# Two value visits of the last head group joined into one burst, with gate loads and softmax sums set behind it

## The chip, the cores and the metric

The kernel runs on one core of one Trainium2 chip. The metric is the device time of one execution in microseconds (us). In the profile's rows PE is TensorE, PEld its weight loads, DVE VectorE, ACT ScalarE, POOL GpSimd and SP the queue that issues nearly all transfers.

## What is computed

One input x of 2048 tokens by 512 goes through two blocks, which a gate per token mixes. Block a is attention with 32 heads of 16 in a causal window of 256 tokens; block b is a gated linear unit with inner size 1376.

```python
def _A_ref(x, wqkv, wo):
    ...
    scores = jnp.einsum("bhqd,bhkd->bhqk", q, k) * (Dh ** -0.5)
    mask = (idx[:, None] - idx[None, :] >= 0) & (idx[:, None] - idx[None, :] < W)
    scores = jnp.where(mask[None, None], scores, -1e9)
    p = _softmax(scores, axis=-1)
    o = jnp.einsum("bhqk,bhkd->bhqd", p, v)
    return (lambda x, *d: x.transpose(*d))(o, 0, 2, 1, 3).reshape(B, S, D) @ wo

def _B_ref(x, w_gate, w_up, w_down):
    ...
    h = _sigmoid(g) * u
    return jnp.einsum("bsf,fd->bsd", h, w_down)

g = _sigmoid((x * gate_w).sum(-1, keepdims=True))
return g * a + (1 - g) * b
```

## The kernel before

Every fp32 product is made of fp32r products of a high and a low part: high by high, high by low, low by high.

**Steps.** The 32 heads are 8 groups of 4, the tokens 16 blocks of 128. One long loop runs over `u` from 0 to 137, a step for each block of each group (group 7 has u 112 to 127) and a few to drain. The order on every engine but POOL is the order in which this code is written. In a step, for each head `hh` of the four: `s_part` (L370) makes a score product of block u with up to two blocks before it, and VectorE takes its row maxima (L376, an instruction and a read-out); nine steps later (`LAG`) `st_part` (L425) makes the transposed scores, with the maxima folded in as extra rows, and ScalarE takes their exponentials (L430) into a buffer, where POOL clears the masked corners (L436, L442). The score products of two heads run side by side in the two halves of TensorE's rows. They end with u 127, the transposed ones with u 136.

**Maxima.** Each four steps the maxima of a chunk of 512 tokens are turned by `max_split` on VectorE (L386, L387, L391), stored, and loaded back by `max_load` into rows of the `ring`, from which the transposed products read them.

**Fillers.** Between the score products stand halves of other products, in pairs side by side as well: projections of the next groups, then the gate and up products (`gu`, L282), and from about u 121 the tail products (`tp`, L612), the last columns of the gate and up matrices and the mixing gate. How many pairs follow each head's scores is read from `GAPS2` (the groups with long bursts) and `GAPS`. ScalarE copies a gate product out; of a tail group VectorE takes a transpose and a copy (L618, L619).

**Value visits.** At step u, `pv_part` (L460) multiplies the exponentials of one chunk with the values, in four column tiles of 32 for the four heads; its 17th row per head is the softmax sum. `visits[u]` is 2 for a long burst of two chunks (chunks of seven head groups, at u 17, 25, to 121) and 1 for single visits (u 125, 129, 133, 137, the last group). A single visit's result is copied out by ScalarE in `o_take` (L471). In a long burst `o_copy` (L478) copies the first half from the bank "pv" and the second from a bank of the tag "st", of which there are two and which the transposed products use in turn; then `o_store` puts the stores in `later`, a list that the next step hands to the SP queue.

**Homes of the exponentials.** `p_home` says where a block's exponentials lie: groups with long bursts use `pbuf` and `pwide`, the last group `pbuf` alone. `pwide` shares its memory with `hv`, the buffer of the gate and up products that come back from DRAM (`h_load`, L757) for the last stage.

**Guests.** `behind` and `acts` hold small work for VectorE and ScalarE that is put in at chosen heads: splits of the down matrix (L136 on ScalarE, L137, the low part, on VectorE) and of wo, and the reciprocals of the softmax sums. `SUMS` says after which step the sums of a chunk are read back (L821), `H_LOAD` when the first gate chunks are.

**The last stage** takes h = sigmoid(g)·u from those chunks (L811, L812), multiplies by the down matrix and by wo, mixes and stores. Its TensorE work is dense and starts behind the tail products.

Of the kernel before, what the change touches and what calls it, by code (L numbers as in the profile page):

```python
# [24 lines left out]
NB = T // P  # L25
# [14 lines left out]
LAG = 9  # L40
PVLAG = LAG + 4
WIDE = 2 * 4
NWIDE = NG - 1
# [3 lines left out]
GAPS = [3] * 12 + [2] * 3  # L47
GAPS2 = [3] * 8 + [2] * 3 + [3] * 10 + [2] * 3 + [3] * 4 + [2] * 3
# [4 lines left out]
TREAD = 133  # L53
WD_LOAD = {119: 0, 120: 1, 121: 2, 122: 3, 128: 4, 129: 5, 131: 6, 132: 7, 135: 8, 136: 9, 137: 10}
WD_SPLIT = {124: 0, 125: 1, 126: 2, 127: 3, 130: 4, 131: 5, 133: 6, 134: 7}
SUMS = {129: 0, 131: 1, 134: 2}
WO = 126
WO_SPLIT = {132: 0, 133: 1, 134: 2, 135: 3}
AHEAD = 7
V_STORE = {2: 0, 3: 1, 6: 2, 10: 3}  # L60
V_LOAD = {122: 7, **{16 * g + 14: g for g in range(7)}}
H_LOAD = {126: (0,), 130: (1, 2), 134: (3, 4), 137: (5, 6)}


@with_exitstack
def gated_mix_kernel(
# [16 lines left out]
    def after(ins, other):  # L83
        tc.add_manual_dep(
            ins.ins, other.ins.name,
            mybir.DependencyInfo(mybir.DependencyClass.Sync, mybir.DependencyReason.DATA), reason="array halves",
        )
# [33 lines left out]
    NU = NG * NB  # L121
# [22 lines left out]
    with ExitStack() as actx:  # L144
# [197 lines left out]
        def run_dmas(dmas):  # L342
            for dst, src in dmas:
                nc.sync.dma_start(dst, src)
# [51 lines left out]
        def max_load(s):  # L396
            st = ring[s // 2 % RING].bitcast(F32).rearrange("(a r) j f -> r a j f", r=QB)
            o = s % 2 * CH
            src = max_d[s].rearrange("a (p s) l b t -> p (s l) b a t", p=2)
            for p in range(2):  # L400
                nc.sync.dma_start(
                    st[0, :, p, o:o + CH].rearrange("r (b a t) -> r b a t", b=4, a=P // QB), src[p],
                )
# [1 line left out]
        homes = (((0, 1), (9, 1), (3, 2), (4, 2)), ((0, 1), (3, 1), (9, 2), (10, 2)))  # L405

        def p_home(u):
            if u // NB >= NWIDE:
                return pbuf, *homes[u // 4 % 2][u % 4]
            if u % WIDE < 4:  # L410
                return pbuf, u % 4 * 3, 1
            return pwide, *homes[u // WIDE % 2][u % 4]
# [38 lines left out]
        def pv_part(s, bank):  # L451
            g, c = divmod(s, NC)
            q0 = 4 * c
            j0 = max(0, q0 - 2)
            for j in range(j0, q0 + 4):
                q, e = max(j, q0), min(j + 3, q0 + 4)
                for hh in range(HG):
                    v = (j * HG + hh) * VW
                    w = min(32, NB * HG * VW - v)
                    mm(  # L460
                        bank[32 * hh:32 * hh + w, (q - q0) * P:(e - q0) * P],
                        vt[:, v:v + w],
                        p_blk(g * NB + j, hh, q - j, e - q),
                        start=j == j0, stop=j == q0 + 3, skip_group_check=True,
                        tile_position=(0, 32 * hh),
                    )
# [238 lines left out]
        def turns():  # L705
            k3 = 3 * ND
            groups = []
            ended = {}
            sizes = GAPS2 * (NB * NWIDE // WIDE) + GAPS + GAPS[0:12]
            sizes += [6] * 14  # L710
            for size in sizes:
                for _ in range(size):
                    t = turns_done[0]
                    turns_done[0] += 1
                    if t % (3 * k3) == 0 and len(groups) < n_rest:
                        groups.extend((work or rest).pop(0) for _ in range(3))
                    for half, v in enumerate((t, t - SHIFT)):
                        if 0 <= v < n_rest * k3:
                            n, k = divmod(v, k3)
                            n += TURN[half][n % 3] - n % 3  # L720
                            ins = groups[n][0](k, half, n in ended)
                            if k == 0 and n in ended and size > 3:
                                after(ins, exps[ended[n]])
                            if k == k3 - 1:
                                if n not in ended:
                                    ended[n] = len(exps)
                                    continue
                                _, behind_it, post = groups[n]
                                if behind_it is None:
                                    post()  # L730
                                else:
                                    evac.append(lambda behind_it=behind_it, post=post: (post(), behind_it()))
                yield
# [108 lines left out]
        def mid(u):  # L842
            return PVLAG <= u < NU and (u - PVLAG) % 4 == 0 and u not in visits

        U_WIDE = NB * NWIDE + LAG
        visits = {u: 2 for u in range(PVLAG + 4, U_WIDE + 1, WIDE)}
        visits.update({u: 1 for u in range(U_WIDE + 4, N, 4)})

# [4 lines left out]
        for u in range(N):  # L853
# [56 lines left out]
            for hh in range(HG):  # L910
                wide = visits.get(u) == 2
                if hh == 0 and u in visits:
                    s2 = (u - PVLAG) // 4 - wide
                    pv_part(s2, pv)
                if hh == 3 and mid(u + 1):
                    max_split((u - 4) // 4)
                if hh == 0 and mark:
                    if not mid(u):
                        max_split((u - 5) // 4)
                    run_dmas(later)  # L920
                    later.clear()
                    max_store((u - 5) // 4)
                if hh == 0 and wide:
                    flush(evac)
                    ripe = [held.pop(0) for _ in range(2) if held and held[0] // 2 == u // 8 + 1]
                    for s4 in ripe:
                        proj_hi(s4)
                    o_copy(0, pv)
                    max_load((u - 5) // 4)
                    for s4 in ripe:  # L930
                        proj_lo(s4)
                    run_dmas(later)
                    later.clear()
                    second = ps.tile([P, CH], F32, tag="st", name=f"pv{s2}", bufs=2)
                    pv_part(s2 + 1, second)
                    for guests, n in ((acts, 2), (behind, 3)):
                        for _ in range(min(n, len(guests))):
                            guests.pop(0)()
                    o_copy(1, second)
                    o_store(s2)  # L940
                elif hh == 0 and u in visits:
                    evac.append(lambda s2=s2: o_take(s2, pv))
                if hh == 2 and mark:
                    transfers()
                if u < NU:
                    s_part(u, hh)
                if 0 <= u - LAG < NU:
                    st_part(u - LAG, hh ^ 1 if u < NU else hh)
                if u < LAG:
                    flush(behind)  # L950
                    if hh % 2 == 1:
                        upto = n_first * (2 * u + 1 + hh // 2) // (2 * LAG)
                        run_first(upto - done)
                        done = upto
                else:
                    long = u < U_WIDE
                    k8 = (u - LAG) % WIDE * HG + hh
                    dense = GAPS2[max(0, k8 - 1)] < 3 if long else u < NU and (u - PVLAG) % 4 == 3 and hh > 0
                    k = (u - PVLAG) % 4 * HG + hh
                    free = hh == 2 and not mid(u + 1) if long else k in (1, 5, 9) or k in (3, 7) and len(behind) > 2  # L960
                    if behind and (u < PVLAG or u >= NU or free):
                        behind.pop(0)()
                    if evac:
                        evac.pop(0)()
                    elif acts and not dense and (u < NU or hh % 2 == 1):
                        acts.pop(0)()
                if u >= LAG and (hh % 2 == 1 or u < NU) and (u + 1 not in visits or hh < HG - 1):
                    if u < N - 2:
                        next(slots)
# [17 lines left out]
            if u in WO_SPLIT:  # L987
                acts.extend(lambda d=d: wo_split(d) for d in range(WO_SPLIT[u], WO_SPLIT[u] + 1))
            if u in SUMS:
                sums_load(SUMS[u])  # L990
            if u - 2 in SUMS:
                behind.append(lambda c=SUMS[u - 2]: later.append(sums_invert(c)))
            if u == TREAD:
                tail_reads(0)
            if u >= TREAD:
                tail_read(0, 2)
            for n in H_LOAD.get(u, ()):
                h_load(n)
# [175 lines left out]
```

## Time and profile before

| | us |
|---|---|
| median of 3 runs | 719.8 (719.02 to 720.11) |
| the profiled execution | 718.91 |
| its span, first to last instruction | 717.2 |
| PE, DVE, ACT, POOL busy | 711.9, 478.3, 430.3, 165.6 |

The granted TensorE clock was 1.000 throughout. Times within the profile count from the span's start. "Idle before" in square brackets is shown from 0.15 us on, with what ended it. A busy TensorE need not be at its peak, since matmuls overlap. Step 121 ends at about 494, the visits of steps 125, 129, 133 and 137 start at 502.08, 516.32, 529.19 and 543.23, and the down product begins at 550.95.

### The profile page before, as it was taken

To read this page: it belongs to the slowest core of one execution; us is meant where nothing else is said; L and a number is where in the kernel's file an instruction comes from. 1 tells how busy PE (TensorE), PEld (TensorE's weight loads), DVE (VectorE), ACT (ScalarE), POOL (GpSimd) and SP (SyncE) were. 2 spreads that over 40 slices of the span, in tenths; PEclk is the share of its full clock that TensorE was granted. 3 is DMA by queue.
4 is the path that set the end of the run, shared out by engine and by line. 5 is a ranking of instruction groups with operands and counts; after the bars stand their busy time and mean duration, and the time that the engine had idled before them with its cause. 6 is when DMAs were issued, how large, how long until landed. Compare 5 with 4: busy or idle time off the path is not lost.

```text
span 717.2 us, 17422 instructions
## 1 busy us (share of the span) xinstructions
PE 711.9 (99%) x6298; PEld 599.9 (84%) x6298; DVE 478.3 (67%) x1455; ACT 430.3 (60%) x890; POOL 165.6 (23%) x254
## 2 busy tenths in 40 slices
PE   9999999999999999999999999999999999999997
PEld 7888879888798798988979888798788888888886
DVE  5368767667676676766667667675837767667481
ACT  6423777677576676767667667775576645435341
POOL 5200333233233233323324323232331000000000
PEclk9999999999999999999999999999999999999999
DMA  8466653736456355562655617574568977879531
GB/s 297 121 183 204 212 180 125 221 100 215 156 174 211 106 186 174 172 217 89 214 160 186 195 55 249 180 237 108 166 203 245 252 204 197 211 168 254 144 65 58
DMA packets 102965, 127.20 MB, mean 177 GB/s; under 512 B 45766, under 2 KB 62662, under 8 KB 102880
## 3 DMA queue, kind: packets, MB, share of 16 engines
q1 hardware_dynamic: 102736, 125.98, 57.9%
q8 instruction: 49, 0.80, 0.5%
q14 instruction: 36, 0.29, 0.1%
q10 hardware_dynamic: 144, 0.13, 0.1%
HBM read 71.80 MB, written 51.13 MB: 171 GB/s over the span
## 4 chain that ended last, share of the span: by engine, by line
PE 98%; DMA 1%; SPq 0%; ACT 0%; issue 0%; DVE 0%; DVEq 0%
PE gu L282 28%; PE pj L282 12%; PE pv L460 11%; PE s L370 6%; PE st L425 6%; PE tp L612 6%; PE pd L96 5%; PE pd L94 5%; PE pd L95 5%; PE vh L649 3%; PE pa L94 2%; PE pa L95 2%; PE pa L96 2%; PE vps L511 1%; DMA V<-in_xT_dram 1%; PE pd L1101 1%
## 5 line engine op out<-in xcount | busy, mean ns | idle before, releaser
L376 DVE CUSTOM_DVE_ANT_0 junk<-s,mask 128x384 f32<-128x384 f32 (+2 forms) x512 | 271.4, 530 | 132.9 <-PE s L370 71.8
L282 PE MATMUL gu<-xh,w 64*128 64x512 f32 x1152 | 271.7, 391 | 0.0
L282 PE MATMUL gu<-xl,w 64*128 64x512 f32 x576 | 183.4, 389 | 0.0
L430 ACT ACTIVATE pbuf<-st 128x384 f32<-128x384 f32 (+2 forms) x288 | 138.3, 490 | 61.1 <-PE st L425 30.7
L425 PE MATMUL st<-ring 64*128 64x384 f32 (+2 forms) x536 | 165.8, 326 | 0.0
L370 PE MATMUL s<-ring 64*128 64x384 f32 (+2 forms) x536 | 162.9, 322 | 0.0
L282 PEld LDWEIGHTS gu<-xh,w 64*128 64x128 f32 x1152 | 153.2, 184 | 7.5
L430 ACT ACTIVATE V<-st 128x384 f32<-128x384 f32 (+2 forms) x224 | 100.5, 454 | 47.6 <-PE s L370 25.1
L370 PEld LDWEIGHTS s<-ring 64*128 64x128 f32 x536 | 94.9, 184 | 15.8 <-issue 3.0
L436 POOL TENSOR_SCALAR_AFFINE_SELECT pbuf<-pbuf 128x512 f32<-128x512 f32 x72 | 46.8, 651 | 253.1 <-ACT pbuf L430 198.9
L425 PEld LDWEIGHTS st<-ring 64*128 64x128 f32 x536 | 95.5, 184 | 3.9 <-PE pv L460 0.4
L282 PEld LDWEIGHTS gu<-xl,w 64*128 64x128 f32 x576 | 89.6, 184 | 2.1
L282 PE MATMUL pj<-xl,wqh 64*128 64x512 f32 (+1 forms) x228 | 79.8, 388 | 0.0
L282 PE MATMUL pj<-xh,wqh 64*128 64x512 f32 (+1 forms) x228 | 79.8, 389 | 0.0
L282 PE MATMUL pj<-xh,wql 64*128 64x512 f32 (+1 forms) x228 | 69.7, 389 | 0.0
L95 PE MATMUL pd<-ring,hb 128*128 128x512 f32 x160 | 62.3, 389 | 0.0
L96 PE MATMUL pd<-ring,hb 128*128 128x512 f32 x160 | 62.3, 389 | 0.0
L94 PE MATMUL pd<-ring,hb 128*128 128x512 f32 x160 | 62.3, 389 | 0.0
L436 POOL TENSOR_SCALAR_AFFINE_SELECT V<-V 128x512 f32<-128x512 f32 x56 | 35.8, 640 | 106.8 <-ACT V L430 102.8
L90 ACT CAST hb<-V 128x512 fp32r<-128x512 f32 x40 | 24.9, 622 | 59.3 <-DVE V L812 47.2
L460 PE MATMUL pv<-pbuf,V 128*32 128x384 f32 (+2 forms) x848 | 49.5, 381 | 0.0
L442 POOL TENSOR_SCALAR_AFFINE_SELECT pbuf<-pbuf 128x512 f32<-128x512 f32 x70 | 44.9, 642 | 0.0
(132 smaller groups left out, 1240.4 us busy)
## 6 DMA issues: line engine op xcount, KB each, us to landing
gu_scratch<-sp SPq DMA_DIRECT2D x72, 256.0 KB
V<-gu_scratch SPq DMA_DIRECT2D x36, 512.0 KB
ring<-stack_scratch SPq DMA_DIRECT2D x56, 256.0 KB
stack_scratch<-sh SPq DMA_DIRECT2D x14, 512.0 KB
stack_scratch<-sl SPq DMA_DIRECT2D x14, 512.0 KB
ring<-stack_scratch SPq DMA_DIRECT2D x14, 512.0 KB
guraw<-in_wgu_dram SPq DMA_DIRECT2D x18, 256.0 KB
v_scratch<-V SPq DMA_DIRECT2D x4, 1088.0 KB
```

Of the source, the lines that this page charges most:

```text
L94: mm(ps, lh, rh, start=first, stop=False)
L95: mm(ps, lh, rl, start=False, stop=False)
L96: mm(ps, ll, rh, start=False, stop=last)
L282: return mm(pt, (wl if w == 2 else wh)[r, d], (xl if w == 1 else xh)[r, d, c * CH:(c + 1) * CH], start=k == 0 and not second, stop=k == 3 ...
L370: mm(pt[:, (k - k0) * P:(e - k0) * P], lhsT, blk(g, k, hh, 1, e - k), start=k == k0, stop=e == i + 1, skip_group_check=True,)
L376: nc.vector.tensor_tensor_reduce(junk[:, 0:n], pt[:, 0:n], mask[:, 3 * P - n:], scale=1.0, scalar=NEG, op0=ALU.add, op1=ALU.max, accum_out ...
L425: mm(pt[:, (q - j) * P:(e - j) * P], lhsT, blk(g, q, hh, 0, e - q), start=q == j, stop=e == last, skip_group_check=True,)
L430: exps.append(nc.scalar.activation(p_blk(u, hh, 0, n), pt[:, 0:n * P].rearrange("p (b t) -> p b t", t=P), AF.Exp, scale=SCALE,))
L436: nc.gpsimd.affine_select(buf[:, s0], buf[:, s0], pattern=[[0, HG], [1, P]], compare_op=ALU.is_ge, fill=0.0, base=0, channel_multiplier=-1,)
L442: nc.gpsimd.affine_select(old, old, pattern=[[0, HG], [-1, P]], compare_op=ALU.is_gt, fill=0.0, base=0, channel_multiplier=1,)
L460: mm(bank[32 * hh:32 * hh + w, (q - q0) * P:(e - q0) * P], vt[:, v:v + w], p_blk(g * NB + j, hh, q - j, e - q), start=j == j0, stop=j == q ...
L612: return mm(tp[b][:, 0:TW], (xl if w == 1 else xh)[r, d, b * P:(b + 1) * P], tw[d][int(w == 2)][r, 0:TW], start=k == 0 and not second, sto ...
```

## The change

The two single visits at u 125 and 129 become one long burst at u 129, as for the other groups. For that blocks 112 to 119 get the homes of the other groups (`pbuf` and `pwide`), and the fillers of the last group the spacing of `GAPS2`. As `pwide` is in use until then, the first gate chunk is loaded at step 130 and no longer at 126, the third at 132 and not 130; the sums of chunks 0 and 1 are read at 130 and 132 and not 129 and 131. At u 129 no maxima are left to load, so `max_load` gets a condition.

```diff
-SUMS = {129: 0, 131: 1, 134: 2}
+SUMS = {130: 0, 132: 1, 134: 2}
...
-H_LOAD = {126: (0,), 130: (1, 2), 134: (3, 4), 137: (5, 6)}
+H_LOAD = {130: (0, 1), 132: (2,), 134: (3, 4), 137: (5, 6)}
...
         def p_home(u):
-            if u // NB >= NWIDE:
+            if u >= NB * NWIDE + WIDE:
                 return pbuf, *homes[u // 4 % 2][u % 4]
...
-            sizes = GAPS2 * (NB * NWIDE // WIDE) + GAPS + GAPS[0:12]
+            sizes = GAPS2 * (NB * NWIDE // WIDE) + GAPS2[0:28]
...
-        U_WIDE = NB * NWIDE + LAG
+        U_WIDE = NB * NWIDE + WIDE + LAG
         visits = {u: 2 for u in range(PVLAG + 4, U_WIDE + 1, WIDE)}
...
                     o_copy(0, pv)
-                    max_load((u - 5) // 4)
+                    if u < NU:
+                        max_load((u - 5) // 4)
```

The order on three places shows it. First VectorE around the last head of step 124. In the rows `junk124_3` is the maximum of step 124 and head 3, `nm30` and `nt30` the turning of the maxima of chunk 30, `tt1` a transpose of tail group 1. Before:

```order
L618 STREAM_TRANSPOSE tt1_8485<-tp1_8342 128x448
L619 COPY gsum_64<-tp1_8342 128x1
L376 ISA junk124_3_8490,mx31_8451<-s124_3_8488,mask_153 128x384
L376 ISA mx31_8451 128x1
L386 TENSOR_SCALAR nm30_8513<-mx30_8157 128x4x4
L387 SCALAR_TENSOR_TENSOR nm30_8513<-mx30_8157,nm30_8513 128x4x4
L391 STREAM_TRANSPOSE nt30_8516<-nm30_8513 128x32
L376 ISA junk125_0_8522,mx31_8451<-s125_0_8520,mask_153 128x384
```

After:

```order
L618 STREAM_TRANSPOSE tt1_8485<-tp1_8342 128x448
L619 COPY gsum_64<-tp1_8342 128x1
L386 TENSOR_SCALAR nm30_8488<-mx30_8157 128x4x4
L387 SCALAR_TENSOR_TENSOR nm30_8488<-mx30_8157,nm30_8488 128x4x4
L391 STREAM_TRANSPOSE nt30_8491<-nm30_8488 128x32
L376 ISA junk124_3_8495,mx31_8445<-s124_3_8493,mask_153 128x384
L376 ISA mx31_8445 128x1
L376 ISA junk125_0_8512,mx31_8445<-s125_0_8510,mask_153 128x384
```

The turning has moved ahead of the maximum of head 3. Further on, the low part of `wdraw2` (L137) has moved from behind the last maximum of step 127 to the place just ahead of it.

Second, TensorE from the same head on (`s124_3` is its score product, `st115_2` a transposed one, `tp` tail products). Before:

```order
L370 MATMUL s124_3_8488<-ring_63 128x384
L425 MATMUL st115_2_8492<-ring_63 128x384
L460 MATMUL pv_869<-pbuf_868,V_71 32x384 x8
L460 MATMUL pv_869<-pbuf_868,V_71 32x256 x4
L460 MATMUL pv_869<-pbuf_868,V_71 32x128 x4
L370 MATMUL s125_0_8520<-ring_63 128x384
L425 MATMUL st116_1_8524<-ring_63 128x384
```

After:

```order
L370 MATMUL s124_3_8493<-ring_63 128x384
L425 MATMUL st115_2_8497<-ring_63 128x384
L612 MATMUL tp2_8373<-tail_hb2_7985,xh_68 128x450
L612 MATMUL tp3_8403<-tail_wqh0_7578,xh_68 128x450
L612 MATMUL tp2_8373<-tail_hb2_7985,xl_69 128x450
L612 MATMUL tp3_8403<-tail_wqh0_7578,xl_69 128x450
L612 MATMUL tp2_8373<-tail_hb2_7985,xh_68 128x450
L612 MATMUL tp3_8403<-tail_wql0_7579,xh_68 128x450
L370 MATMUL s125_0_8510<-ring_63 128x384
L425 MATMUL st116_1_8514<-ring_63 128x384
```

The visit between steps 124 and 125 is gone, and a filler turn that was left out ahead of it stands there.

Third, TensorE at step 129, with what each row waits for. After (`pv28` is the second half's bank):

```order
L460 MATMUL pv28_8758<-V_71 32x128 [waits Activation_49] x3
L425 MATMUL st120_0_8786<-ring_63 128x384 [waits PE_49]
L425 MATMUL st120_1_8789<-ring_63 128x384 [waits Activation_49]
L612 MATMUL tp7_8792<-tail_wqh0_7578,xh_68 128x450 [waits DVE_49]
L612 MATMUL tp6_8601<-tail_hb2_7985,xh_68 128x450
```

Before, at the same place:

```order
L460 MATMUL pv_869<-pbuf_868,V_71 32x128 [waits Activation_49] x3
L425 MATMUL st120_0_8791<-ring_63 128x384 [waits PE_49]
L425 MATMUL st120_1_8796<-ring_63 128x384 [waits PE_49]
L612 MATMUL tp7_8799<-tail_wqh0_7578,xh_68 128x450 [waits DVE_49]
L612 MATMUL tp6_8631<-tail_hb2_7985,xh_68 128x450
```

The product of head 1 now follows ScalarE, which has the second half's copy ahead in its row.

## The prediction

> **What bounds the kernel now.** I read the first part of the page, then the chain of waits.
>
> ```profile
> PE 711.9 (99%) x6298; PEld 599.9 (84%) x6298; DVE 478.3 (67%) x1455; ACT 430.3 (60%) x890; POOL 165.6 (23%) x254
> ...
> PE 98%; DMA 1%; SPq 0%; ACT 0%; issue 0%; DVE 0%; DVEq 0%
> ```
>
> TensorE (PE) is busy for 711.9 of 717.2 us and holds 98% of the chain. That reads as "whatever shortens TensorE's list shortens the kernel". But a share over the whole span says nothing about one stage, so the second view is a table by stretch: one between two long bursts, then the stretch between the visits of steps 125 and 129, then one after 129. Columns: length, then busy time of PE, PEld, DVE, ACT, POOL, clock, DMA.
>
> ```profile
> 459.71:484.53 24.82, 24.82 (x239) 23.66 (x236) 18.37 (x67) 17.71 (x40) 7.97 (x13) 1.00 0.72 231
> ...
> 504.16:516.07 11.91, 11.91 (x124) 10.90 (x120) 10.31 (x36) 8.88 (x19) 3.66 (x6) 1.00 0.58 178
> 519.05:528.93 9.88, 9.88 (x104) 9.28 (x100) 3.19 (x8) 7.27 (x17) 3.72 (x6) 1.00 0.60 160
> ```
>
> VectorE (DVE) is 74% busy in the first (18.37 of 24.82), 87% in the second, 32% in the third, where no score maxima are left. In the second, TensorE's fillers are the tail products, each of whose groups costs VectorE a transpose and a copy, where the earlier gate products were evacuated by ScalarE. Even 87% is less than the truth, as VectorE's timeline there shows (start, length, engine, line, tile):
>
> ```profile
> 490.53 0.56 DVE L376 CUSTOM_DVE_ANT_0 junk<-s,mask 128x384 f32<-128x384 f32 x1 [4.24 <-PE s L370]
> ...
> 494.78 0.56 DVE L376 CUSTOM_DVE_ANT_0 junk<-s,mask 128x384 f32<-128x384 f32 x1
> ...
> 495.48 0.65 DVE L618 STREAM_TRANSPOSE tt<-tp 128x448 f32<-128x448 f32 x1
> ...
> 496.10 0.54 DVE L376 CUSTOM_DVE_ANT_0 junk<-s,mask 128x384 f32<-128x384 f32 x1
> ...
> 496.80 0.56 DVE L376 CUSTOM_DVE_ANT_0 junk<-s,mask 128x384 f32<-128x384 f32 x1
> ...
> 497.50 0.56 DVE L376 CUSTOM_DVE_ANT_0 junk<-s,mask 128x384 f32<-128x384 f32 x1
> ...
> 502.89 0.54 DVE L376 CUSTOM_DVE_ANT_0 junk<-s,mask 128x384 f32<-128x384 f32 x1
> ...
> 503.37 0.17 DVE L386 TENSOR_SCALAR nm<-mx 128x16 fp32r<-128x16 f32 x1
> ...
> 504.09 0.21 DVE L391 STREAM_TRANSPOSE nt<-nm 128x32 f32<-128x32 f32 x1
> 504.63 0.56 DVE L376 CUSTOM_DVE_ANT_0 junk<-s,mask 128x384 f32<-128x384 f32 x1 [0.34 <-PE s L370]
> ...
> 508.98 0.08 DVE L376 DVE_READ_ACCUMULATOR2_ANT mx<- 128x1 f32 x1
> 509.20 0.56 DVE L376 CUSTOM_DVE_ANT_0 junk<-s,mask 128x384 f32<-128x384 f32 x1
> ...
> 509.69 0.69 DVE L137 TENSOR_TENSOR ring<-wdraw,ring 128x512 fp32r<-128x512 f32 x1
> 510.29 0.55 DVE L376 CUSTOM_DVE_ANT_0 junk<-s,mask 128x384 f32<-128x384 f32 x1
> ...
> 514.20 0.56 DVE L376 CUSTOM_DVE_ANT_0 junk<-s,mask 128x384 f32<-128x384 f32 x1
> ```
>
> From 496.10 on one maximum follows the other every 0.70 us with no wait named between them: a maximum costs VectorE 0.70 us, not the 0.56 of its row. The one rest is the 0.34 us at 504.63, behind the visit of step 125. And TensorE does wait:
>
> ```profile
> 509.11 0.18 PEld L370 LDWEIGHTS s<-ring 64*128 64x128 f32 x1 [0.30 <-DVE mx L376]
> ...
> 510.90 0.18 PEld L370 LDWEIGHTS s<-ring 64*128 64x128 f32 x1 [0.31 <-DVE mx L376]
> ```
>
> A score product takes the bank of the second maximum before it: the read-out ending at 509.06 (508.98 and 0.08) lets the product start at 509.11. So between steps 121 and 128 two engines run level, and the value visit at step 125 is the pause in which VectorE catches up.
>
> **The change part by part.** Its visits stand like this in TensorE's timeline (the long burst of step 121, then 125, then 129):
>
> ```profile
> 484.68 0.86 PE L460 MATMUL pv<-V 128*32 128x128 f32 x16
> ...
> 490.00 0.32 PE L370 MATMUL s<-ring 64*128 64x128 f32 x1
> ...
> 491.03 0.34 PE L425 MATMUL st<-ring 64*128 64x384 f32 x1
> ...
> 501.81 0.34 PE L370 MATMUL s<-ring 64*128 64x384 f32 x1
> 502.08 2.15 PE L460 MATMUL pv<-pbuf,V 128*32 128x384 f32 x32
> ...
> 504.16 0.44 PE L370 MATMUL s<-ring 64*128 64x384 f32 x1
> ...
> 516.32 2.80 PE L460 MATMUL pv<-pbuf,V 128*32 128x128 f32 x48
> ...
> 519.05 0.44 PE L425 MATMUL st<-ring 64*128 64x384 f32 x2
> ```
>
> *The visit at 125 goes.* From its first product to the next other one are 2.08 us. With its switch (0.27 from the last score product, of which about half is ordinary spacing) and a cold restart some 2.3 us leave TensorE's list ahead of step 129. They come out of the time only if VectorE needs less, too. VectorE's groups between 490.5 and 514.7 (count, then busy time and mean ns):
>
> ```profile
> L376 DVE CUSTOM_DVE_ANT_0 junk<-s,mask 128x384 f32<-128x384 f32 x28 | 15.5, 554 | 8.3 <-PE s L370 5.8 <-PE st L425 0.5
> L618 DVE STREAM_TRANSPOSE tt<-tp 128x448 f32<-128x448 f32 x5 | 3.2, 646 | 0.2
> ...
> L137 DVE TENSOR_TENSOR ring<-wdraw,ring 128x512 fp32r<-128x512 f32 x2 | 1.4, 687 | 0.0
> ```
>
> The fifth transpose stands behind the last maximum. VectorE's need from the first maximum at 490.53 to the last at 514.20, before: 27 spacings of 0.70 are 18.9; the four transposes before it with their copies at 0.62 (495.48 to 496.10), 2.5; two low parts, each lengthening a spacing from 0.70 to 1.09 (509.20 to 510.29), 0.8; one turning of the maxima, 0.93 (503.37 to 504.30) and 0.48 ahead of it instead of 0.70, so 0.7. Together 22.9 of 23.67 us; most of the rest is at the start, where five spacings to 494.78 take 4.25 instead of 3.5, and there the change moves nothing. After, VectorE has the same 28 maxima, the same four transposes, the same turning (now ahead of the last maximum of step 124 and no longer under a visit), and one low part more, the third, ahead of the last maximum: plus 0.39. Its pause of 0.34 goes. So the last maximum comes between 0.0 and 0.4 us later than before, not 2.3 earlier. All that follows it up to the visit (step 128) is unchanged, so the visit of 129 starts **0.2 us later** (ends: minus 2.3, if VectorE holds nothing; plus 0.4).
>
> Here a rule bears on it: the Trainium skill, TensorEngine Tiling (Array Packing), PSUM Bottleneck, says that packing the array speeds up TensorE but not the emptying of PSUM, which may then become the bottleneck. By the busy row of TensorE (11.91 of 11.91) the term would be minus 2.3; by that rule it is about nothing. The two waits on VectorE side with the rule.
>
> *The visit at 129 becomes a burst of both.* Joined visits save a little: the two of step 121 take 5.32 (484.68 to 490.00), two like that of 129 (516.32 to 519.05, 2.73) would be 5.46. So 2.08 and 2.73 less 0.14 are 4.67 in place of 2.73: **plus 1.94** (ends 1.9 and 2.1).
>
> *The second half's bank.* The second half is summed in a bank of the tag "st", of which there are two, and is copied out by ScalarE. The score product of step 129 for head 1 takes that bank next and must wait for the copy. Before, it followed the visit at once. In the long bursts with score rows still to come this copy is covered by some 1 us of other work (the product that takes the bank stands at 491.03, TensorE went on at 490.00); at 129 only one product for head 0 stands ahead. The price is from the copy at 121:
>
> ```profile
> 490.14 0.58 ACT L478 COPY pbuf<-pv 128x512 f32<-128x512 f32 x1 [2.00 <-PE pv L460]
> ```
>
> It starts 0.14 after TensorE went on, takes 0.58, and a release costs about 0.05 (509.06 to 509.11): **plus 0.77**. Queued behind the waiting product is all of TensorE. Below, 0.5 if the other half of the array works on; above, 1.3 if the weight cast queued on ScalarE between the two copies runs late, but the second half's 2.6 us cover it.
>
> *Gate loads and sums.* The first gate load moves from step 126 to 130, the second stays, the third goes from 130 to 132; the first two sums go one step later. On the SP queue the first sums now follow their own store and hold the queue until it has landed, as the third do now:
>
> ```profile
> 510.90 1.40 SPq L757 DMA_DIRECT2D V<-gu_scratch  x1
> ...
> 535.52 0.53 SPq L344 DMA_DIRECT2D sum_scratch<-ob  x1
> 537.24 0.34 SPq L821 DMA_DIRECT2D sm<-sum_scratch  x1
> ...
> 543.14 0.63 ACT L811 ACTIVATE V<-V 128x512 f32<-128x512 f32 x1
> ```
>
> That is 1.7 us from store to load, with two gate loads and a weight load behind it. The first user of a gate load is at 543.14, some 15 us after the new place of the load. **Nothing**, with that cover; without it, up to 2. The larger stores replace two sets of smaller ones: nothing.
>
> The sum is 0.2, 1.94 and 0.77: **plus 2.9**. Nothing gives it back, since TensorE has no idle time to lose behind it. The profiled execution took 718.9 us (span 717.2, 1.7 around it), so 721.8; the median shown, 719.8, lies 0.9 above it, so 722.7 on that scale.
>
> **The rivals.** *TensorE sets the pace* (not slower): VectorE's spacing shrinks when products come faster, the 2.3 us come out, and what stays is minus 2.3, plus 1.94, plus 0.77, or plus 0.4: 720.2. For it speaks the 99%; against it that 0.70 us appears exactly where VectorE waits for nobody. It decides if a maximum costs less than about 0.63 us on average (2 us saved over 27).
>
> *One switch saved, and no more* (faster, by little): as before, but the copy is hidden: minus 0.4, 719.4. The Trainium skill, TensorEngine Tiling (Array Packing), Key Properties, has TensorE drained at each change of tiling mode, so one burst saves a drain. The row of 502.08 prices a change at some 0.3. Against it: only one product stands between the burst and the bank.
>
> *The queue holds the gate* (slower still): sums, store and gate loads pile up on SP and the gate comes late for step 136; plus 2 on top, 724.7. It decides only if the loads are more than 15 us late; the landing in the rows is 1.7.
>
> That the change isn't what it says is no rival: both orders show the burst.
>
> **How the numbers follow.** Forecast 0.82, TensorE's pace 0.11, one switch 0.03, the queue 0.04. The forecast's own ends: 0.0 to 0.4, 1.9 to 2.1 and 0.5 to 1.3 give plus 2.4 to 3.8, and the runs differ by half a microsecond either way: 721.7 to 724.0. Down to 720.2 the range takes in the first rival. 0.2% (1.4 us) is about what a measurement of this kernel can tell from no change; faster by more than that nothing here reaches (0.02), within it are the first two rivals and a tenth of doubt (0.14), slower are the others (0.84).
>
> **What would show it.** In the profile after: no L460 between the bursts of 121 and 129, more waits of PEld L370 for DVE mx there (some 2 us in sum, the longest behind the turning L386), the burst starting near 516.5 instead of 514, lasting 4.7, and one wait of PEld st L425 for ACT pbuf L478 of about 0.8. Wrong would be a burst that starts near 514: then the first rival holds.

## The result, and the profile after

The changed kernel took 723.48 us (median, 722.7 to 724.62), the kernel before 719.41 in the same runs: ratio 1.005, 95% interval 1.0034 to 1.0067. The forecast was 722.7, made up of 719.8 and 2.9; the difference measured here is 4.07. The profiled execution took 723.39 (span 721.3), the one before 718.91 (717.2): 4.1 more in span where the sum said 2.9.

The page after, first part and chain of waits:

```profile
PE 713.8 (99%) x6298; PEld 600.2 (83%) x6298; DVE 478.6 (66%) x1455; ACT 431.0 (60%) x890; POOL 165.0 (23%) x254
...
PE 97%; DVE 1%; issue 0%; DMA 0%; DVEq 0%; ACT 0%
```

TensorE is as full as before; 1% of the chain has gone to VectorE. TensorE's timeline after: the end of the burst of step 121, the burst of 129, the single visits of 133 and 137.

```profile
485.76 0.86 PE L460 MATMUL pv<-V 128*32 128x128 f32 x16
...
491.08 0.32 PE L370 MATMUL s<-ring 64*128 64x128 f32 x1
...
517.57 2.80 PE L460 MATMUL pv<-pbuf,V 128*32 128x384 f32 x48
520.18 2.12 PE L460 MATMUL pv<-V 128*32 128x384 f32 x32
522.24 0.44 PE L425 MATMUL st<-ring 64*128 64x384 f32 x1
523.09 0.44 PE L425 MATMUL st<-ring 64*128 64x384 f32 x1 [0.41 <-ACT pbuf L478]
...
533.23 0.86 PE L460 MATMUL pv<-V 128*32 128x128 f32 x16
...
547.26 2.80 PE L460 MATMUL pv<-pbuf,V 128*32 128x128 f32 x48
```

The visit of 137 before, for comparison:

```profile
543.23 2.80 PE L460 MATMUL pv<-pbuf,V 128*32 128x128 f32 x48
```

Counted from the end of the burst of 121 (490.00 before, 491.08 after), the burst of 129 starts at 26.49 (26.32 before): +0.17. It takes 4.67 (517.57 to 522.24) for 2.73: +1.94. The product that needs the copied bank comes 0.85 behind the burst. The visit of 137 stands at 56.18 for 53.23, +2.95, and from there to the end 0.1 is added. The rest of the 4.1, 1.08, lies ahead of step 121, where both programs are the same. It is mainly one wait for a load of maxima (0.69 on TensorE, 0.99 on its weight loads); SP's timeline and TensorE's there, after:

```profile
444.25 0.40 SPq L394 DMA_DIRECT2D max_scratch<-nt  x1
448.30 1.18 SPq L401 DMA_DIRECT2D ring<-max_scratch  x2
```

```profile
450.45 0.41 PE L425 MATMUL st<-ring 64*128 64x384 f32 x1 [0.69 <-DMA ring<-max_scratch]
```

The load waits for the store: 4.05 from one to the other. Before it was 2.71, without a wait:

```profile
444.23 0.36 SPq L394 DMA_DIRECT2D max_scratch<-nt  x1
446.94 1.18 SPq L401 DMA_DIRECT2D ring<-max_scratch  x2
```

Waits of the weight loads behind the burst of 121, after (total, times, longest):

```profile
PEld s L370 <- DVE mx L376: 3.9, 10, 1.1
...
PEld st L425 <- ACT pbuf L478: 0.7, 1, 0.7
```

Before there were two on VectorE, of 0.30 and 0.31. VectorE's timeline after, around the turning of the maxima:

```profile
502.85 0.56 DVE L376 CUSTOM_DVE_ANT_0 junk<-s,mask 128x384 f32<-128x384 f32 x1
...
503.42 0.65 DVE L618 STREAM_TRANSPOSE tt<-tp 128x448 f32<-128x448 f32 x1
...
504.04 0.15 DVE L386 TENSOR_SCALAR nm<-mx 128x16 fp32r<-128x16 f32 x1
504.23 0.62 DVE L387 SCALAR_TENSOR_TENSOR nm<-mx,nm 128x16 fp32r<-128x16 f32 x1
504.88 0.21 DVE L391 STREAM_TRANSPOSE nt<-nm 128x32 f32<-128x32 f32 x1
505.02 0.52 DVE L376 CUSTOM_DVE_ANT_0 junk<-s,mask 128x384 f32<-128x384 f32 x1
```

Here is TensorE's longest wait, for the maximum behind the turning:

```profile
505.60 0.18 PEld L370 LDWEIGHTS s<-ring 64*128 64x128 f32 x1 [1.06 <-DVE mx L376]
```

### The profile page after: what moved, and what is told of

Same layout as the page of the kernel before. It is cut to its first block, busy times and chain, and to the rows that moved or that the text cites. A ratio compares the mean times of both kernels' runs of the same rounds, so it can differ in the third digit from the quotient of the medians.

```text
span 721.3 us, 17415 instructions
## 1 busy us (share of the span) xinstructions
PE 713.8 (99%) x6298; PEld 600.2 (83%) x6298; DVE 478.6 (66%) x1455; ACT 431.0 (60%) x890; POOL 165.0 (23%) x254
## 4 chain that ended last, share of the span: by engine, by line
PE 97%; DVE 1%; issue 0%; DMA 0%; DVEq 0%; ACT 0%
PE gu L282 28%; PE pj L282 12%; PE pv L460 11%; PE st L425 6%; PE s L370 6%; PE pd L95 5%; PE pd L96 5%; PE pd L94 5%; PE tp L612 5%; PE vh L649 3%; PE pa L94 2%; PE pa L96 2%; PE pa L95 2%; PE vps L511 2%; DVE junk L376 1%; PE pd L1102 1%
## 5 line engine op out<-in xcount | busy, mean ns | idle before, releaser
L425 PE MATMUL st<-ring 64*128 64x384 f32 (+2 forms) x536 | 167.9, 327 | 1.1 <-DMA ring<-max_scratch 0.7
L430 ACT ACTIVATE pbuf<-st 128x384 f32<-128x384 f32 (+2 forms) x272 | 130.6, 490 | 55.2 <-PE st L425 27.7
L430 ACT ACTIVATE V<-st 128x384 f32<-128x384 f32 (+2 forms) x240 | 108.3, 457 | 53.8 <-PE s L370 27.5
L436 POOL TENSOR_SCALAR_AFFINE_SELECT pbuf<-pbuf 128x512 f32<-128x512 f32 x68 | 43.9, 645 | 247.3 <-ACT pbuf L430 228.5
L436 POOL TENSOR_SCALAR_AFFINE_SELECT V<-V 128x512 f32<-128x512 f32 x60 | 38.5, 641 | 117.0 <-ACT V L430 112.9
L460 PE MATMUL pv<-pbuf,V 128*32 128x384 f32 (+2 forms) x800 | 46.7, 381 | 0.0
L282 PEld LDWEIGHTS pj<-xh,wql 64*128 64x128 f32 (+1 forms) x228 | 41.4, 184 | 1.9
```

Source lines behind the costliest of these rows:

```text
L282: return mm(pt, (wl if w == 2 else wh)[r, d], (xl if w == 1 else xh)[r, d, c * CH:(c + 1) * CH], start=k == 0 and not second, stop=k == 3 ...
L425: mm(pt[:, (q - j) * P:(e - j) * P], lhsT, blk(g, q, hh, 0, e - q), start=q == j, stop=e == last, skip_group_check=True,)
L430: exps.append(nc.scalar.activation(p_blk(u, hh, 0, n), pt[:, 0:n * P].rearrange("p (b t) -> p b t", t=P), AF.Exp, scale=SCALE,))
L436: nc.gpsimd.affine_select(buf[:, s0], buf[:, s0], pattern=[[0, HG], [1, P]], compare_op=ALU.is_ge, fill=0.0, base=0, channel_multiplier=-1,)
L460: mm(bank[32 * hh:32 * hh + w, (q - q0) * P:(e - q0) * P], vt[:, v:v + w], p_blk(g * NB + j, hh, q - j, e - q), start=j == j0, stop=j == q ...
```

## The experiments

All are set against the kernel before in the same runs. Columns 2 to 4 come from one profile each: the end of the burst of 121, and counted from it the start of the visit or burst of 129 and the visit of 137. In this way the wait near 450 falls out.

| kernel | burst of 121 ends | 129 | 137 | median | before | ratio, 95% |
|---|---|---|---|---|---|---|
| before | 490.00 | 26.32 | 53.23 | | | |
| changed | 491.08 | 26.49 | 56.18 | 723.48 | 719.41 | 1.005 (1.0034 to 1.0067) |
| changed, again | 491.51 | 26.51 | 56.19 | 722.82 | 719.53 | 1.0035 (1.002 to 1.005) |
| changed, other bank | 491.71 | 26.51 | 55.37 | 722.94 | 719.53 | 1.0039 (1.0024 to 1.0055) |
| changed, lighter maxima | 490.62 | 24.18 | 53.88 | 720.55 | 719.53 | 1.0005 (0.9994 to 1.0015) |
| before, lighter maxima | 492.14 | 25.87 | 52.77 | 719.43 | 719.53 | 0.9991 (0.9977 to 1.0005) |
| changed, bank and lighter | 491.26 | 24.21 | 53.06 | 719.47 | 719.74 | 0.9996 (0.9986 to 1.0007) |
| changed, bank and threes | 490.14 | 25.85 | 54.28 | 721.62 | 719.74 | 1.0023 (1.0011 to 1.0034) |
| before, tail loads later | 489.78 | 26.31 | 53.21 | 719.59 | 719.74 | 0.9998 (0.999 to 1.0007) |
| changed, tail loads later | 489.54 | 26.52 | 56.21 | 722.16 | 719.74 | 1.0033 (1.002 to 1.0046) |
| changed, bank, threes, GpSimd | 489.71 | 25.57 | 54.01 | 721.23 | 719.66 | 1.002 (1.0011 to 1.0029) |
| before, sums and gate loads | 489.91 | 26.32 | 53.24 | 720.1 | 719.66 | 1.0009 (1.0 to 1.0017) |
| before, threes | 491.53 | 26.86 | 55.42 | 721.93 | 719.66 | 1.0031 (1.0019 to 1.0042) |
| before, two junk buffers | 488.52 | 25.91 | 52.83 | 717.41 | 719.52 | 0.9972 (0.9961 to 0.9983) |

**The changed kernel again.**

> The changed kernel once more, nothing edited. It asks about the microsecond that the changed kernel's profile shows ahead of step 121 (one wait of a score product at 450.45 us, behind a store of maxima that landed late: 3.5 us from store to load at 426.56, where before had 1.5), in a part where the two programs are the same. Theory A, chance of that one execution: the profile shows no such wait at that place, the long burst of step 121 starts within 0.2 us of before's 484.68, the span is 717.2 + 3.0 = 720.2 (from the terms +0.17, +1.94 and +0.85 read after step 121), and the ratio to before is 1.004. Theory B, it belongs to the change: the same wait of 1 us near 450 again, burst of 121 at 485.8, span 721.3, ratio 1.0055.

```profile
450.82 0.18 PEld L425 LDWEIGHTS st<-ring 64*128 64x128 f32 x1 [1.93 <-issue]
```

The wait came again, longer, so theory A in its simple form fell. But B falls with the lighter *kernel before*, whose profile has it too:

```profile
451.47 0.18 PEld L427 LDWEIGHTS st<-ring 64*128 64x128 f32 x1 [1.78 <-issue]
```

Over all profiles with the loads in their old place it is there in eight of twelve: in just those where the load is issued 3.7 us or more behind the store. Six of the seven kernels with the joined burst have it and two of the five with single visits. The code is the same up to there, so no way is seen in which the change could cause it, but twelve profiles don't settle whether it comes more often behind the change. Behind step 121 the repeat agrees with the first profile within 0.02.

The repeat has one more wait, in the last stage: a down product waits 0.39 at 572.34. It is taken up below, with the gate loads.

**The other bank.**

```diff
-                    second = ps.tile([P, CH], F32, tag="st", name=f"pv{s2}", bufs=2)
+                    second = ps.tile([P, CH], F32, tag="st" if u < NU else "s", name=f"pv{s2}", bufs=2)
```

> The changed kernel with one word changed: the second half of the burst at step 129 is summed in a bank of the tag s (free by then, since the last score maximum is through) in place of a bank of the tag st. Theory, the wait for the copy: the wait of the st product for ScalarE's copy (0.67 in the trace, 0.85 from the end of the burst to the product) is gone, the burst itself stays at 4.67, the visit of step 133 comes 0.8 earlier counted from the end of the burst of step 121 (41.35 in place of 42.15), the end 0.7 to 0.9 us earlier: ratio to before 1.003 where the changed kernel has 1.004 to 1.0055. Rival, ScalarE itself is late there (the copy stands between exponentials whichever bank it reads): the wait comes back one or two products later at the same price, no gain, under 0.2 us.

```profile
518.22 2.80 PE L460 MATMUL pv<-pbuf,V 128*32 128x384 f32 x48
520.84 2.12 PE L460 MATMUL pv<-V 128*32 128x384 f32 x32
522.89 0.44 PE L425 MATMUL st<-ring 64*128 64x384 f32 x2
```

Both products start at the burst's end. The visit of 133 stands at 41.33 (42.15), that of 137 0.81 earlier: the theory, to 0.01. The median shows none of it (722.94 for 722.82): this profile had the wait near 450 with 1.5 us, the intervals are some 2 us wide, and 0.8 is too small for them.

**Lighter maxima, in the changed kernel and in the one before.**

```diff
+            kept = 1 if u > NU - 8 else i + 1 - k0
...
-            n = (i + 1 - k0) * P
+            n = kept * P
+            off = (i + 1 - k0 - kept) * P
...
-                junk[:, 0:n], pt[:, 0:n], mask[:, 3 * P - n:], scale=1.0, scalar=NEG,
+                junk[:, 0:n], pt[:, off:off + n], mask[:, 3 * P - n:], scale=1.0, scalar=NEG,
```

> The changed kernel in which the score maxima of steps 121 to 127 are taken over the newest 128 of the 384 columns (left out: the maximum over the two older blocks; the maximum is only subtracted ahead of the exponential). A maximum over 128x128 has a row of 0.29 us in the profile before, one over 128x384 0.56. Theory, VectorE holds the stretch: the last maximum and with it the burst of step 129 come 1.9 to 3.1 us earlier, counted from the end of the burst of step 121 (23.4 to 24.6 in place of 26.49), waits of PEld L370 for DVE mx in the stretch are nearly gone (3.9 us in 10 now), and the end comes 1.9 to 3.1 us earlier. Rival, TensorE sets the pace: under 0.4 us of change, burst at 26.1 to 26.5.

> The kernel before with the same lighter maxima in steps 121 to 127 (left out: the maximum over the two older blocks). Theory, VectorE holds the stretch but the visit of step 125 gives it the time back: TensorE loses its few waits only, the visit of step 129 comes 0.3 to 0.8 us earlier (25.5 to 26.0 from the end of the burst of step 121 in place of 26.32), the end as much. With the changed kernel's light version at the forecast's other sum (minus 2.3 plus 1.94 plus 0.77), the two light versions then lie 0.4 us apart where the kernels themselves lie 3.0 apart. Rival, TensorE sets the pace: the two light versions lie 3.0 us apart like the kernels.

Waits behind the burst of 121, changed kernel with lighter maxima:

```profile
PEld s L371 <- DVE mx L378: 0.8, 1, 0.8
PEld st L427 <- ACT pbuf L480: 0.7, 1, 0.7
```

Nine of the ten waits are gone, and the burst starts 2.31 earlier (24.18 for 26.49); the kernel before gains 0.45. That is VectorE's hold by itself: with it the visit at 125 could be taken away without gain. The 1.11 between the light versions is not the 0.4 of the sum, because one wait of 0.8, behind the turning, is left in one and not in the other, which turns under its visit. Both light versions leave out part of the maxima, so they are probes and not kernels to keep.

**Both edits.**

> The changed kernel with both edits: the other bank for the second half and the lighter maxima in steps 121 to 127 (left out: the maximum over the two older blocks). If the two terms are independent, counted from the end of the burst of step 121 the visit of step 137 stands at 56.18 - 0.82 - 2.31 = 53.05 (the kernel before: 53.23; before with the lighter maxima: 52.77), so the joined burst is then worth what it is on TensorE's list alone, with one wait of 0.4 to 0.8 left behind the turning of the maxima. Median 2.9 to 3.4 below the changed kernel's 722.8, so 719.4 to 719.9. Rival, the two waits cover for each other (one wait gone lets the other grow): 53.5 or more.

Measured 53.06 for 53.05, and 719.47 for 719.4 to 719.9: the terms add up. What joining is worth by itself must be read against the kernel before with the same lighter maxima, 52.77: the joined burst is 0.29 later, with one wait of 0.79 for VectorE left behind the turning. Whether it would win something without that wait is open.

**More fillers ahead of the burst ("the threes").**

```diff
-            sizes = GAPS2 * (NB * NWIDE // WIDE) + GAPS2[0:28]
+            sizes = GAPS2 * (NB * NWIDE // WIDE) + [3] * 28
```

> The changed kernel with the other bank, and three product pairs of filler instead of two in every slot of the last half head group (28 threes, six pairs of TensorE's list moved from behind the burst of step 129 to ahead of it; one tail group more ends there, so VectorE has one transpose and one copy more, 0.62, ahead of the last maximum). Theory, VectorE holds the stretch and TensorE has idle time there: the burst of step 129 starts 0.5 to 0.7 later (27.0 to 27.2 from the end of the burst of 121; 26.51 without the six pairs), and behind it about 1.2 us of list are gone (six pairs at 0.2), so the visit of 137 comes 0.5 to 0.7 earlier than 55.37. Rival, TensorE's list sets the time: the burst starts 1.2 later, 27.7, and 137 stays at 55.4.

A miss for both theories: the burst came 0.66 *earlier* than without the six pairs, though VectorE had a transpose more. Its last maximum came 0.30 earlier (24.24 for 24.54 from the end of the burst of 121), and its timeline shows how that can be; the other 0.36 lies between the last maximum and the burst and isn't explained.

```profile
512.21 0.56 DVE L376 CUSTOM_DVE_ANT_0 junk<-s,mask 128x384 f32<-128x384 f32 x1
512.69 0.08 DVE L376 DVE_READ_ACCUMULATOR2_ANT mx<- 128x1 f32 x1
512.69 0.64 DVE L618 STREAM_TRANSPOSE tt<-tp 128x448 f32<-128x448 f32 x1
...
513.30 0.54 DVE L376 CUSTOM_DVE_ANT_0 junk<-s,mask 128x384 f32<-128x384 f32 x1
```

A transpose starts 0.48 behind a maximum, and the next maximum 1.09 behind the first: it costs 0.39, not the 0.62 that the prediction took for all of them. Which guests meet decides: in the changed kernel a transpose and the turning lay together, 502.85 to 505.02 from one maximum to the next, 1.47 above 0.70. Of that, 0.45 is one instruction of the turning (L387), which took 0.62 there and here 0.17:

```profile
503.32 0.17 DVE L387 SCALAR_TENSOR_TENSOR nm<-mx,nm 128x16 fp32r<-128x16 f32 x1
```

So VectorE's need was not a fixed sum of rows. The 1.09 won at 137 did not reach the end in this profile: later, in the last stage, a down product waited 1.40 for VectorE, some 10 us behind a gate activation that had waited 2.80 for its load.

**The tail loads one step later.**

```diff
-TAIL_LOAD = {109: 0, 110: 1, 114: 2, 115: 3}
-TAIL_SPLIT = {110: 0, 111: 1, 116: 2, 117: 3}
+TAIL_LOAD = {110: 0, 111: 1, 114: 2, 115: 3}
+TAIL_SPLIT = {111: 0, 112: 1, 116: 2, 117: 3}
```

> The kernel before with the first two tail weight loads and their splits one step later (110 and 111 for 109 and 110; 111 and 112 for 110 and 111): the first was issued just ahead of the store of maxima at step 109, the one whose landing is late in five of the six profiles so far (from store to load 4.0 to 4.9 us, 2.7 in the other), with a wait of 1.0 to 1.9 us on TensorE near 450. Theory, the load's traffic holds the store: store to load at that place 2.7 or less, no wait near 450, the median 0.3 to 1.0 under the kernel before, and the spread of the spans smaller (before: 716.7 to 719.2 in 32 of 35). Rival, chance of the queues with or without that load: no change of the median or spread, and a wait at the same place in the profile as likely as not.

> The changed kernel with the same shift of the two tail weight loads. Theory, the load's traffic holds the store of maxima: no wait near 450, span 717.2 + 3.0 - 0.0 = 720.2 or less in most runs, median 0.8 to 1.5 under the changed kernel's 722.8. Then the difference of the two shifted kernels is the 3.0 us read behind step 121, with no other part. Rival: like the changed kernel, 722.8 within 0.5.

Neither profile has the long wait (store to load 2.99 and 2.21; 0.22 at that place in the first, nothing in the second), and the spans of the two differ by 2.7. But 719.59 for 719.74 is no gain, and 722.16 (of five runs) for 722.8 is under what can be told. Two profiles without a wait don't settle whether the load's traffic was the cause; that stays open.

**Low parts on GpSimd, besides the threes.**

```diff
-        low = lambda: nc.vector.tensor_tensor(lo, raw, hi.bitcast(F32), op=ALU.subtract)
+        eng = nc.gpsimd if f < 3 and late else nc.vector
+        low = lambda: eng.tensor_tensor(lo, raw, hi.bitcast(F32), op=ALU.subtract)
```

> The changed kernel with the other bank, the threes of the run with the moved fillers, and the low parts of the first three down weight chunks on GpSimd in place of VectorE (three products of 128x512 that stand between the last twelve score maxima). In the run with the threes each of them lengthens a maximum's spacing on VectorE from 0.70 to 1.08. Theory, VectorE still holds the stretch from the turning of the maxima on: 3 times 0.38, 1.1 us off VectorE, of which TensorE can use what it waits there (four waits of 0.3 to 0.4, some 0.7 above ordinary spacing); the visit of step 137 comes 0.4 to 1.0 earlier than 54.28 from the end of the burst of 121. The kernel before stands at 53.23. Rival, GpSimd and VectorE get in each other's way (in the changed kernel a product of 128x16 on VectorE took 0.62 in place of 0.18 beside a GpSimd select): no gain, 54.2 or more, with rows of VectorE lengthened beside the GpSimd products.

It gained 0.27, less than the theory's 0.4. A low part takes GpSimd about 1.3 us, but VectorE's maxima beside it stay at 0.54 to 0.56, so the rival's cause doesn't show; three waits on VectorE are left, 1.0 in all, and the third last maximum waits 0.28 for TensorE's score.

**Only the sums and gate loads, in the kernel before.**

```diff
-SUMS = {129: 0, 131: 1, 134: 2}
+SUMS = {130: 0, 132: 1, 134: 2}
...
-H_LOAD = {126: (0,), 130: (1, 2), 134: (3, 4), 137: (5, 6)}
+H_LOAD = {130: (0, 1), 132: (2,), 134: (3, 4), 137: (5, 6)}
```

> The kernel before with only the last part of the change: the gate loads at 130, 130, 132 and the sums at 130, 132 instead of 126, 130, 130 and 129, 131; visits as before. Theory, nothing: visits at 125, 129, 133, 137 within 0.1 of 12.08, 26.32, 39.19, 53.23 from the end of the burst of step 121, no wait of ScalarE or VectorE for a gate load at the first gate activation, median within 0.5 of before. Rival, the SP queue holds the gate: the end 1 to 2 us later, behind a gate load or a sum that landed late.

On TensorE nothing, to 0.01. On ScalarE there is something: the sixth gate activation waits for its load, which the kernel before doesn't have. The same wait in this run and in the changed kernel:

```profile
556.57 0.63 ACT L811 ACTIVATE V<-V 128x512 f32<-128x512 f32 x1 [0.92 <-DMA V<-gu_scratch]
```

```profile
561.30 0.63 ACT L811 ACTIVATE V<-V 128x512 f32<-128x512 f32 x1 [1.54 <-DMA V<-gu_scratch]
```

All nine profiles with the moved sums and gate loads have it, with 0.60 to 2.80, and none of the five without. So moving them does make a later gate load late. Up to 1.92 it cost TensorE nothing; behind 2.54 (the repeat) and 2.80 (the threes) a down product waited, 0.39 and 1.40, some 10 us later. The chain from the one to the other wasn't followed. The median lies 0.4 above (1.0009, interval from 1.0), at the edge of what can be told.

**The threes in the kernel before.**

```diff
-            sizes = GAPS2 * (NB * NWIDE // WIDE) + GAPS + GAPS[0:12]
+            sizes = GAPS2 * (NB * NWIDE // WIDE) + [3] * 27
```

> The kernel before, visits unchanged, with three product pairs in every slot of the last half head group (three pairs more ahead of the last maximum, 0.6 us of TensorE's list moved forward; no tail group more ends there). Theory, VectorE holds only the two waits after the turning (0.30 and 0.31, some 0.25 above ordinary spacing) and TensorE's list the rest: the visit of 129 comes 0.3 to 0.6 later than 26.32, that of 137 0.0 to 0.4 earlier than 53.23; median within 0.5 of before. It is the candidate for a kernel that beats both; by this sum it can't be told from before.

The visit of 129 came 0.54 later as expected, that of 137 2.19 later, a miss. Behind the visit of 129 stand waits that the kernel before doesn't have:

```profile
PEld tp L612 <- ACT pbuf L430: 1.8, 5, 0.6
```

The code makes the second half of a tail group wait for an exponential; that the three moved pairs bring it there too soon is argued, not tested. The candidate lost.

**Two buffers for the discarded output.** The threes had shown that a maximum holds VectorE 0.48 us when another kind of work follows, and 0.70 when a maximum does.

```diff
-            junk = spool.tile([P, 3 * P + 16], F32, tag="junk", name=f"junk{u}_{hh}", bufs=1)
+            junk = spool.tile([P, 3 * P + 16], mybir.dt.bfloat16, tag="junk", name=f"junk{u}_{hh}", bufs=2)
```

> The kernel before with the discarded output of each score maximum (the tile junk) in two buffers of half the width (bf16) in place of one in fp32; the maxima themselves are written as before. In the program each maximum waits for VectorE's own maximum before it, since both write the one buffer; without a wait the next instruction of VectorE starts 0.48 behind a maximum's start (502.64 to 503.11, 512.21 to 512.69 in the run with the threes), while the next maximum starts 0.70 behind it. Theory, the 0.22 between is that wait: the spacing of maxima that follow each other falls from 0.70 to about 0.5, the waits of PEld L370 for DVE mx in the stretch between the bursts go as with the lighter maxima (visit of 129 at 25.9 and of 137 at 52.8 from the end of the burst of 121, 26.32 and 53.23 before), the other waits of this kind (2.2 us in nine places ahead of step 121, some 0.2 each ordinary spacing) shrink too, and the median is 0.4 to 1.0 under the kernel before. It is the candidate for a kernel that beats both, though by less than one measurement can tell for certain. Rival, the 0.22 is the engine's own (the read-out of the accumulator has to end): spacing 0.70 as before, all times within 0.1 and the median within 0.3.

```profile
494.62 0.54 DVE L376 CUSTOM_DVE_ANT_0 junk<-s,mask 128x384 bf16<-128x384 f32 x1
495.09 0.08 DVE L376 DVE_READ_ACCUMULATOR2_ANT mx<- 128x1 f32 x1
495.09 0.55 DVE L376 CUSTOM_DVE_ANT_0 junk<-s,mask 128x384 bf16<-128x384 f32 x1
...
508.38 0.55 DVE L376 CUSTOM_DVE_ANT_0 junk<-s,mask 128x384 bf16<-128x384 f32 x1
508.85 0.09 DVE L376 DVE_READ_ACCUMULATOR2_ANT mx<- 128x1 f32 x1
508.85 0.56 DVE L376 CUSTOM_DVE_ANT_0 junk<-s,mask 128x384 bf16<-128x384 f32 x1
```

Where the next score is ready, a maximum now starts 0.47 behind the one before it. The rows of the maxima are as long as before; the edit also halves the width of the output, and no run changes the number of buffers alone. That a wait has gone shows in VectorE's queue, which records semaphore instructions at this line 480 times in the kernel before and 50 times in this one:

```profile
L376 DVEq EVENT_SEMAPHORE  x480: 21/21/21, 40.0 to 514.1; - x160
```

```profile
L376 DVEq EVENT_SEMAPHORE  x50: 21/21/21, 39.4 to 490.9; - x50
```

The waits of the score products for VectorE, over the whole run, in this kernel and then in the one before:

```profile
PEld s L370 <- DVE mx L376: 0.8, 4, 0.2
```

```profile
PEld s L370 <- DVE mx L376: 2.9, 11, 0.4
```

The visits come at 25.91 and 52.83 (25.9 and 52.8 expected). The median, 717.41 for 719.52, is a gain of 2.1, more than the 0.4 to 1.0 expected; the burst of 121 ends earlier too, by 1.0 or more, than in any other profile. It beats both kernels. The joined burst with this edit was not run.

## Why the prediction was right

**The visit at 125.** The term +0.2 measured +0.17, and its mechanism was shown by the pair of lighter versions: 2.31 us lay ready on TensorE's list and VectorE held them. That 99% of TensorE's time was busy said nothing of it. The Trainium skill's rule (TensorEngine Tiling (Array Packing), PSUM Bottleneck), that emptying PSUM may become the limit, fits: with lighter emptying the burst moved by 2.31. The score products' waits for VectorE came to 3.9 in sum, not some 2, the longest behind the turning, as forecast.

That the size came so near is luck in part. The reason given, "0.70 us appears exactly where VectorE waits for nobody", was wrong in part: VectorE did wait, for its own maximum before, in a wait that the rows don't name, and 0.22 of the 0.70 was that. The 0.34 at 504.63 was not its one rest either: the rows name 0.18 at 500.38 and 0.22 at 505.43 too. And 0.62 for each transpose was a size off. In the profile before, two of the four cost 0.39 and 0.40, the first of them here (1.09 from one maximum to the next):

```profile
501.80 0.56 DVE L376 CUSTOM_DVE_ANT_0 junk<-s,mask 128x384 f32<-128x384 f32 x1
...
502.28 0.64 DVE L618 STREAM_TRANSPOSE tt<-tp 128x448 f32<-128x448 f32 x1
...
502.89 0.54 DVE L376 CUSTOM_DVE_ANT_0 junk<-s,mask 128x384 f32<-128x384 f32 x1
```

In the changed kernel some guests cost less than the prediction's prices and a transpose with the turning more (1.47 for 1.32). From 495.86 to 515.59 all of them come to 4.33 above 22 spacings of 0.70, where the prices give 4.35: the errors cancelled. The last maximum came 0.31 later (24.51 for 24.20 from the end of the burst of 121), and the way from it to the burst, which the prediction took as unchanged, was 0.14 shorter.

**The burst.** 4.67 for 2.73, +1.94, to the digit.

**The bank.** +0.77 forecast, 0.85 measured, 0.82 won back by the other bank.

**Gate loads and sums.** Nothing on TensorE in the first profile of the changed kernel and in the run with them alone; 0.39 in the repeat. The cover of 15 us was reckoned for the first gate loads, and there it held. The prediction did not look at the later ones, where the sixth gate activation now waits.

**The rivals.** TensorE's pace fell with the lighter versions: the burst began at 517.57, near the 516.5 forecast plus the 1.08 ahead of it, not at 514. "One switch saved" needed the copy to be hidden, and it wasn't: 0.85. With the other bank it was hidden, but VectorE still held the burst (its start at 26.51, the visit of 137 at 55.37 for 53.23). Whether a saved switch is worth the 0.4 stays open, since in the light pair, too, one wait for VectorE is left in the joined burst. The queue's 2 us did not come; a gate load did come late, with nothing, 0.39 and, with the threes, 1.40 on TensorE.

**The total.** 2.95 on the path for 2.9. The 1.08 on top in the profiled execution goes with a late store, in a part where the code is the same. The medians moved by 4.07 in the first measurement and by 3.29 in the repeat, and the intervals (2.4 to 4.8 and 1.4 to 3.6) hold 2.9 in both. The forecast of 722.7 stands as near to 723.48 as it does partly because its base of 719.8 was 0.4 above the 719.41 of the same runs.

## What to carry to other kernels

Taking work off a full engine paid nothing here, as the engine that empties its results had no room: look at the stage, and lighten the other engine alone to see what lies ready. When work is joined, ask which buffer its result sits in and who needs that buffer next; a free bank of another tag took out 0.8 here. When loads are moved, follow the ones behind them too, up to their last user. Where equal instructions follow each other at a constant spacing longer than the gap to other work, look for a shared output, even a discarded one.

## What the hardware showed

- A wait of VectorE for its own last instruction cost 0.22 us per maximum (0.70 with one output buffer, 0.47 to 0.48 with two). The Trainium skill, VectorE: DVE Perf Modes, The DRAIN you can't avoid, found a semaphore after each copy to cost nothing extra; for a maximum with its read-out the runs say otherwise, and they decide. (The run with two buffers also halved the output's width.)
- A 128x16 instruction of VectorE (L387) took 0.62 at 504.23 beside a GpSimd select of the same time. In the run with the threes the select started behind it, at 503.59, and it took 0.17 (503.32). The select in the changed kernel:

```profile
504.19 0.64 POOL L436 TENSOR_SCALAR_AFFINE_SELECT pbuf<-pbuf 128x512 f32<-128x512 f32 x1 [1.91 <-PE tp L612]
```

  The Trainium skill, SBUF — State Buffer, Who interferes with whom, calls their shared ports an exclusive lock; these rows agree, though no run took the select away.
- From one and the same small store to the load behind it lay 2.2 to 5.0 us in the fourteen profiles. In the eight with 3.7 or more, the weight loads of TensorE stood still for 0.6 to 1.9 us at the product that needs that load; in the six with 3.2 or less, for 0.22 at most.
